# Attention plus a dense eight-expert MLP on one core: one shared ring for the factors of x, expert groups that begin with two pairs, and a planner with new engine costs

## The chip, the cores and the metric

The kernel runs on one core of a Trainium2 chip. The metric is the device time of one execution in microseconds (us). The kernel before takes 2119.99 us, the median of three runs (2118.72 to 2120.39).

The engines are named as in the profile: PE (TensorE matmuls) and PEld (its weight loads), DVE (VectorE), ACT (ScalarE), POOL (GpSimd) and SP (SyncE, which only issues DMAs here). Each works through its own queue in order and waits for the others by semaphores.

## What is computed

The input x has 2048 rows of 512. With xn the layer norm of x, the output is x + attention(xn) + experts(xn):

```python
# attention: 32 heads of 16, a window of 256 keys
qkv = xn @ wqkv
scores = q @ k.T * 16 ** -0.5         # masked to 0 <= row - key < 256
o = softmax(scores) @ v
A = o @ wo
# experts: all 8 take part (K = 8 of E = 8), F = 1376
gates = softmax(xn @ w_gate)
B = sum(gates[:, e] * (silu(xn @ w1[e]) @ w2[e]) for e in range(8))
```

All inputs are f32. The kernel splits each operand of a matmul into a high and a low half of f16 and adds three products (high by high, high by low, low by high), which the helper `mm3` issues.

## The kernel before

**Phase 0** (about the first 130 us) normalises x in four blocks of 512 rows (`tb`), projects queries, keys and values, and writes to DRAM what the second phase reads: the stacked queries and keys, the values, and the seven factors of each block of x (`XS`, 7 parts of 256 KB).

**The expert work** takes the 86 pairs of 128-column chunks of w1 and w2 in 17 *groups*. A group is two or three pairs of one expert (one group mixes chunks that lie across two experts). For a pair and a block of rows the first product, w1 by x, is one step of Strassen's method: seven products (`product`) of a combination of w1's quarters (`w`) with one factor of x (`xs`), held in two PSUM banks `zx` and `zy`, and combined by copies and additions on ACT, DVE and POOL (`s`, `za`, `zb`). Two such units run together as a *double*; `first_products` issues a double's seven products in the order p1, p2, p6, p5, p7, p3, p4. In a group of two pairs each of its four doubles is both pairs of one block of rows. In a group of three pairs, six doubles: pairs 0 and 1 of block tb, then pair 2 of blocks tb and tb + 1 (the *two-block double*), then pairs 0 and 1 of block tb + 1.

A finished unit gives two *rows* (`row`): tanh on ACT (`t`, L628), the gate of silu on DVE (L632), the high half `hh` on ACT (L643) and the low half `hl` on POOL (L646). When all rows of a group and block are there, `second` issues the second product on PE into banks `acc`, and DVE adds each bank to the output block (`x`, L568).

**The attention** runs beside it: 384 *items* of scores (`st` on PE), exponentials on ACT (`pf`, L1717), masks on POOL (L1701, L1708), high half `ph` on ACT (L1723), low half `pl` on DVE (L1727), then products with the values (`pv`). Separate products `sc` find the row maxima on DVE (L1624).

**The order on every engine is made by a planner** (`Order`) at build time. It keeps a modelled time for PE and a modelled clock for A (ACT), V (DVE), G (POOL) and S (SP). `task` queues work for an engine with a cost, dependencies and a due time; `advance` takes from each queue what can start. The PE stream asks `wait(needs)` before each product: while the needs are not met in the model, it puts other work ahead (second products, attention). The real order is what the planner emits; the real waits are by semaphores.

**Loads of x's factors.** `load_x_part` (L508 to L519) issues one part when the part it replaces has been read. Each of the seven parts has its own tag with two buffers (`xs0` to `xs6`, L517), 14 places of 2 KB per partition; a part is replaced by the same part two blocks later.

**Weights.** Each pair of w1 and w2 is loaded twice (`r`, one buffer each): once for the group's largest value (ACT, L839), once to be split and summed (`prep1`: `sums` on POOL, `w` on ACT and DVE). `hh` and `hl` have HB = 12 buffers each, w2 has 8 places.

Of the kernel before, what the change touches and what calls it, by code (L numbers as in the profile page):

```python
# [47 lines left out]
HB = 12  # L48
# [11 lines left out]
UNITS = 24000  # L60

# [19 lines left out]
class Order:  # L81
# [3 lines left out]
    def __init__(self):  # L85
        self.t = 0
        self.clock = {"A": 0, "V": 0, "G": 0, "S": 0}
        self.todo = {e: [] for e in self.clock}
        self.n = 0
        self.idle = 0  # L90
        self.strict = True

    def task(self, engine, cost, run, deps, slack, lag=0):
        ev = Event()
        self.n += 1
        self.todo[engine].append((self.t + slack, self.n, cost, lag, run, deps, ev))
        return ev
# [15 lines left out]
    def advance(self):  # L113

        while True:
            best = None
            for engine, todo in self.todo.items():
# [3 lines left out]
                for job in todo:  # L121
                    e = self.at(job[5])
                    if e is not None:
# [12 lines left out]
            self.todo[engine].remove(job)  # L136
            job[4]()
            self.clock[engine] = start + job[2]
            job[6].end = start + job[2] + job[3]
# [16 lines left out]
def tile_attn_moe(ctx: ExitStack, tc: tile.TileContext, x, wqkv, wo, _bx, wg, w1, w2, out):  # L156
# [158 lines left out]
    def prep1(g, i, r1, slot, act, dve, gps):  # L315
# [46 lines left out]
        e1 = gps(805, s1, [])  # L362
        e2 = gps(805, s2, [e1])
        h = act(500, part(a11, 0, 0, 2), [])
        w[A11] = dve(694, part(a11, 1, 0, 2), [h])
        h = act(712, part(both, 0, 6, 4), [e2])
        low = dve(867, part(both, 1, 6, 4), [h])
        w[S1] = w[S2] = low
        e4 = gps(915, s4, [e2, low])
        e3 = gps(915, s3, [e4])  # L370
        h = act(712, part(rest, 0, 2, 4), [])
        w[A12] = w[A22] = dve(904, part(rest, 1, 2, 4), [h])
        h = act(712, part(both, 0, 10, 4), [e3])
        w[S4] = w[S3] = dve(867, part(both, 1, 10, 4), [h])

    def prep2(g, i, j, r2, slot, act, dve):
# [12 lines left out]
        w["done"] = dve(838, low, [act(712, high, [])])  # L389
# [18 lines left out]
    order = Order()  # L408

# [98 lines left out]
    ahead = [0] * 7  # L508

    def load_x_part(m, free, slack):  # L510

        if ahead[m] < len(blocks):
            b = blocks[ahead[m]]
            ahead[m] += 1

            def run():
                t = moe.tile([P, 2, 2, TB // 2], F16, tag=f"xs{m}", name=f"xs{m}_{b[0]}_{b[1]}")  # L517
                nc.sync.dma_start(t, XS[b[1]][:, m])
                xs[(*b, m)] = t  # L519

            xs_at[(*b, m)] = order.move(1, run, free + ([xs_at[(*blocks[ahead[m] - 2], m)]] if ahead[m] > 1 else []), slack, LOADED)
# [20 lines left out]
    def second(g, tb, a):  # L542
# [35 lines left out]
        evicted[i_bank] = added[tb, a] = order.task("V", 746, add, deps, 6000)  # L578
# [34 lines left out]
    def row(unit, v, r, which, deps, slack):  # L613
# [31 lines left out]
        def low():  # L645
            nc.gpsimd.tensor_tensor(out=h["lo"], in0=h["t"], in1=h["hi"], op=ALU.subtract)  # L646

        before = [t_gone[-2]]
        t = order.task("A", 714, tanh, [*deps, ready[g], last_row, *before], slack)
        s = order.task("V", 805, silu, [t], slack + 1000)  # L650
        read = s
        if mixed:
            ld = order.move(2, gate_load, [gated_at[0]], slack - 3000, LOADED)
            s = order.task("V", 706, gate, [s, ld], slack + 4000)
# [4 lines left out]
        h["high"] = order.task("A", 627, high, [s, *before], slack + 2000)  # L659
        h["low"] = order.task("G", 1262, low, [h["high"]], slack + 3000)  # L660
# [23 lines left out]
    def first_products(d):  # L684
# [8 lines left out]
        def product(ps, m, n, start, stop, needs):  # L693
# [15 lines left out]
            for b in sorted({(g, tb) for g, i, tb in units}):  # L709
                if uses[b] == d:  # L710
                    load_x_part(n, [ev], 8000)
# [32 lines left out]
        def fourth():  # L744
# [9 lines left out]
        s1 = order.task("A", 588, copy(X, tile_s1), [p1, s1_gone], 2500)  # L754
        p2 = product(Y1, A12, B21, True, True, [zgone[by]])
        za0 = s1_gone = order.task(
            "V", 682, add(Y1, lambda: z_tile("a")[:, :, early], lambda: Z["s"]), [p2, s1, *reads_a], 2500
        )
        p6 = product(X, S2, T2, False, False, [s1])
        za1 = order.task("A", 588, copy(X, lambda: Z["a"][:, :, late]), [p6, za0], 2500)  # L760
        p5 = product(Y2, S1, T1, True, False, [za0])
        zb1 = order.task("V", 683, scale_y, [p5, *reads_b], 2500)
        p7 = product(X, S3, T3, False, False, [za1])
        zb0 = order.task("A", 588, copy(X, lambda: Z["b"][:, :, early]), [p7, zb1], 2500)
# [1179 lines left out]
```

## Time and profile before

| what | value |
|---|---|
| median of 3 runs | 2119.99 us |
| the profiled execution | 2119.92 us, span 2117.9 us, 2.0 us around the span |
| PE | 2093.1 us busy (99%), 16916 matmuls |
| DVE | 1625.3 us (77%) |
| ACT | 1367.1 us (65%) |
| POOL | 979.9 us (46%) |
| HBM traffic | 130 GB/s over the span |

A busy PE in this profile counts each matmul from its start to a modelled end. Successive matmuls overlap, so how fast PE works is read from the distance between starts, and what PE lost is read from its idle time and the waits that ended it. Where the text names a wait, the time is that of the engine named first, and what stands behind the arrow is what ended the wait.

### The profile page before, as it was taken

How to read it: one execution, taken by the hardware profiler on the slowest of the kernel's cores; microseconds unless marked ns; L12 is line 12 of the kernel's file. 1: busy time of each engine (PE TensorE's matmuls, PEld its weight loads, DVE VectorE, ACT ScalarE, POOL GpSimd, SP SyncE). 2: the span in 40 equal slices, each digit the busy share in tenths (PEclk: the TensorE clock that was granted, in tenths of full speed). 3: DMA queues.
4: the chain of work that ended last, by engine and by line, in shares of the span. 5: the costliest groups of instructions: out<-in, count | busy, mean ns of one | idle time of the engine just before them, and what ended most of it. 6: DMA issues, size and time to landing. Idle time of an engine off the chain costs nothing.

```text
span 2117.9 us, 44861 instructions
## 1 busy us (share of the span) xinstructions
PE 2093.1 (99%) x16916; PEld 1419.3 (67%) x16916; DVE 1625.3 (77%) x3505; ACT 1367.1 (65%) x2454; POOL 979.9 (46%) x1050
## 2 busy tenths in 40 slices
PE   7999999999999999999999999999999999999999
PEld 4656666666676667666676666666666676666674
DVE  8757787877787787778798878778787877887763
ACT  5747667666675576666666676667676666756561
POOL 4634454445352545355354535445454445444441
PEclk9999999999999999999999999999999999999999
DMA  6875444433533453434554444534444334544311
GB/s 211 282 235 176 136 132 144 118 113 110 155 106 119 130 145 106 132 101 135 158 152 145 117 131 120 149 99 137 110 129 137 107 104 116 159 127 112 78 51 50
DMA packets 287817, 279.15 MB, mean 132 GB/s; under 512 B 128328, under 2 KB 189768, under 8 KB 287600
## 3 DMA queue, kind: packets, MB, share of 16 engines
q1 hardware_dynamic: 287600, 276.28, 45.1%
q8 instruction: 133, 2.18, 0.4%
q14 instruction: 84, 0.69, 0.1%
HBM read 250.42 MB, written 25.50 MB: 130 GB/s over the span
## 4 chain that ended last, share of the span: by engine, by line
PE 94%; DVE 2%; DMA 2%; ACT 1%; issue 1%; SPq 0%; POOL 0%; DVEq 0%; POOLq 0%; ACTq 0%
PE acc L164 14%; PE acc L165 14%; PE acc L166 14%; PE zx L164 7%; PE zx L166 7%; PE zx L165 7%; PE zy L164 5%; PE zy L166 5%; PE zy L165 5%; PE st L1761 4%; PE pv L1798 3%; PE sc L1636 3%; PE qk L1342 3%; PE vg L1405 2%; DMA r<-in_B_w_dram 1%; PE wo L166 1%
## 5 line engine op out<-in xcount | busy, mean ns | idle before, releaser
L646 POOL TENSOR_TENSOR hl<-t,hh 128x512 f16<-128x512 f32 x344 | 436.8, 1278 | 348.2 <-ACT hh L643 332.2
L164 PE MATMUL acc<-w,hh 128*128 128x512 f16 x1376 | 521.1, 379 | 2.1 <-DVE x L568 2.1
L166 PE MATMUL acc<-w,hl 128*128 128x512 f16 x1376 | 521.3, 379 | 0.0
L165 PE MATMUL acc<-w,hh 128*128 128x512 f16 x1376 | 521.2, 379 | 0.0
L164 PE MATMUL zx<-xs,w 128*128 128x256 f16 x1376 | 374.8, 272 | 1.9 <-ACT s L725 1.1
L166 PE MATMUL zx<-xs,w 128*128 128x256 f16 x1376 | 374.9, 272 | 0.0
L165 PE MATMUL zx<-xs,w 128*128 128x256 f16 x1376 | 374.9, 272 | 0.0
L1717 ACT ACTIVATE pf<-st,esc 128x512 f32<-128x512 f32 (+1 forms) x384 | 251.2, 657 | 183.5 <-PE st L1761 177.7
L1624 DVE CUSTOM_DVE_ANT_0 sc<-sc,mask 128x320 f32<-128x320 f32 (+4 forms) x512 | 240.6, 474 | 136.2 <-PE sc L1636 132.4
L1727 DVE TENSOR_TENSOR pl<-pf,ph 128x512 f16<-128x512 f32 (+1 forms) x384 | 301.9, 792 | 50.1 <-ACT ph L1723 48.6
L164 PEld LDWEIGHTS <-w 128*128 128x128 f16 x2408 | 235.0, 98 | 106.2 <-DVE za L732 0.3
L165 PEld LDWEIGHTS <-w 128*128 128x128 f16 x2408 | 235.2, 98 | 95.2 <-issue 5.3
L164 PE MATMUL zy<-xs,w 128*128 128x256 f16 x1032 | 281.1, 272 | 2.5 <-DVE za L732 2.2
L166 PE MATMUL zy<-xs,w 128*128 128x256 f16 x1032 | 281.2, 273 | 0.0
L165 PE MATMUL zy<-xs,w 128*128 128x256 f16 x1032 | 281.2, 272 | 0.0
L1723 ACT ACTIVATE ph<-pf 128x512 f16<-128x512 f32 (+1 forms) x384 | 228.7, 598 | 49.2 <-POOL pf L1701 29.4
L166 PEld LDWEIGHTS <-w 128*128 128x128 f16 x2408 | 235.4, 98 | 27.4
L643 ACT ACTIVATE hh<-t 128x512 f16<-128x512 f32 x344 | 213.6, 623 | 57.7 <-DVE t L632 42.1
L1701 POOL TENSOR_SCALAR_AFFINE_SELECT pf<-pf 128x256 f32<-128x256 f32 x256 | 132.3, 518 | 249.3 <-ACT pf L1717 248.5
L166 PEld LDWEIGHTS <-hl 128*128 128x128 f16 x1376 | 134.3, 98 | 162.6
L568 DVE SCALAR_TENSOR_TENSOR x<-acc,gsc,x 128x512 f32<-128x512 f32 x256 | 190.3, 743 | 69.0 <-PE acc L166 66.8
L746 POOL TENSOR_TENSOR zb<-zb 128x512 f32<-128x512 f32 x86 | 113.6, 1321 | 230.8 <-ACT zb L725 183.9
(144 smaller groups left out, 3679.5 us busy)
## 6 DMA issues: line engine op xcount, KB each, us to landing
xs<-XS SPq DMA_DIRECT2D x476, 256.0 KB
r<-in_B_w_dram SPq DMA_DIRECT2D x172, 256.0 KB
r<-in_B_w_dram SPq DMA_DIRECT2D x80, 512.0 KB
q<-QS SPq DMA_DIRECT2D x192, 32.0 KB
VS<-vt SPq DMA_DIRECT2D x16, 272.0 KB
out_dram<-x SPq DMA_DIRECT2D x16, 256.0 KB
k<-KS SPq DMA_DIRECT2D x96, 40.0 KB
x<-in_A_x_dram SPq DMA_DIRECT2D x3, 1024.0 KB
```

Of the source, the lines that this page charges most:

```text
L164: nc.tensor.matmul(ps, lhsT=lh, rhs=rh, start=first, stop=False, **kw)
L165: nc.tensor.matmul(ps, lhsT=lh, rhs=rl, start=False, stop=False, **kw)
L166: nc.tensor.matmul(ps, lhsT=ll, rhs=rh, start=False, stop=last, **kw)
L568: nc.vector.scalar_tensor_tensor(out=dst, in0=ps, scalar=back if groups[g][0] is None else back[:, 4 * tb + a : 4 * tb + a + 1], in1=dst, ...
L643: nc.scalar.activation(out=h["hi"], in_=h["t"], func=AF.Copy)
L646: nc.gpsimd.tensor_tensor(out=h["lo"], in0=h["t"], in1=h["hi"], op=ALU.subtract)
L746: nc.gpsimd.tensor_tensor(out=zb[:, :, late], in0=zb[:, :, early], in1=zb[:, :, late], op=ALU.add)
L1624: nc.vector.tensor_tensor_reduce(out=ps[:, :n], in0=ps[:, :n], in1=maskf[:, MB * 64 - n :], scale=1.0, scalar=-3.0e38, op0=ALU.add, op1=AL ...
L1701: nc.gpsimd.affine_select(out=pf, in_=pf, pattern=[[0, 2], [1, P]], channel_multiplier=-1, base=0, compare_op=ALU.is_ge, fill=0.0,)
L1717: nc.scalar.activation(out=w["pf"][:, :n], in_=ps[:, :n], func=AF.Exp, bias=math.log(PSCALE), scale=esc)
L1723: nc.scalar.activation(out=w["hi"][:, :n], in_=w["pf"][:, :n], func=AF.Copy)
L1727: nc.vector.tensor_tensor(out=w["lo"][:, :n], in0=w["pf"][:, :n], in1=w["hi"][:, :n], op=ALU.subtract)
```

## The change

1. *One ring for x's factors.* The seven tags with two buffers become one tag `xs` with XB = 10 buffers. Parts are loaded in the order in which the products read them, block after block, and each load takes the place of the part loaded ten loads earlier. In phase 0 the 16 tiles of normalised x use the same ring.
2. *Buffers.* HB goes from 12 to 13, and w2 gets 11 places in place of 8.
3. *Groups.* Experts 0 to 6 are cut into a group of two pairs and then one of three, in place of three and then two. Expert 7 was cut so already.
4. *Low halves on either engine.* `hl` and `pl` are queued for DVE and POOL at once (`either`); the one that the model can start first takes it, and DVE only where POOL's modelled queue could not finish it in time (`in_time`).
5. *Costs.* The planner's costs for ACT, DVE, POOL and some PE work are changed (ACT's by some 100 ns each, for example tanh from 714 to 618), and a result now counts as ready LATE (80 to 100 ns) after its engine is free.

```diff
-HB = 12
+HB = 13
+XB = 10
+W2B = 11
...
+LATE = {"A": 100, "V": 80, "G": 80}
...
+    def in_time(self, job):
+
+        due, n = job[:2]
+        ahead = sum(j[2] for j in self.todo["G"] if j[:2] <= (due, n) and self.at(j[5]) is not None)
+        return max(self.clock["G"], self.at(job[5])) + ahead <= max(due, self.t + 2000)
+
+    def either(self, costs, run, deps, slack):
+
+        ev = Event()
+        self.n += 1
+        self.twins[self.n] = [
+            (engine, (self.t + slack, self.n, cost, 0, partial(run, engine), deps, ev)) for engine, cost in costs.items()
+        ]
+        for engine, job in self.twins[self.n]:
+            self.todo[engine].append(job)
         return ev
...
-                    if e is not None:
+                    if e is not None and not (engine == "V" and job[1] in self.twins and self.in_time(job)):
...
-            self.todo[engine].remove(job)
+            for e, twin in self.twins.pop(job[1], [(engine, job)]):
+                self.todo[e].remove(twin)
             job[4]()
             self.clock[engine] = start + job[2]
-            job[6].end = start + job[2] + job[3]
+            job[6].end = start + job[2] + (job[3] if engine == "S" else LATE[engine])
...
-        groups += [(e, pairs[:3]), (e, pairs[3:])] if e < E - 1 else [(e, pairs[:2]), (e, pairs[2:])]
+        groups += [(e, pairs[:2]), (e, pairs[2:])]
...
-    def load_x_part(m, free, slack):
-
-        if ahead[m] < len(blocks):
...
+    x_todo = iter([(b, m) for b in blocks for m in ORDER])
+    x_issued = Event(0)
+
+    def load_x_part(free, slack):
+
+        nonlocal x_issued
+        b, m = next(x_todo, (None, None))
+        if b is None:
+            return
+        before, x_issued = x_issued, Event()
+        here = x_issued
+
+        def run():
+            t = moe.tile([P, 2, 2, TB // 2], F16, tag="xs", bufs=XB, name=f"xs{m}_{b[0]}_{b[1]}")
+            nc.sync.dma_start(t, XS[b[1]][:, m])
+            xs[(*b, m)] = t
+            here.end = order.clock["S"] - AGO
+
+        xs_at[(*b, m)] = order.move(1, run, [*free, before], slack, LOADED)
...
-        t = order.task("A", 714, tanh, [*deps, ready[g], last_row, *before], slack)
-        s = order.task("V", 805, silu, [t], slack + 1000)
+        t = order.task("A", 618, tanh, [*deps, ready[g], last_row, *before], slack)
+        s = order.task("V", 730, silu, [t], slack + 1000)
...
-        h["high"] = order.task("A", 627, high, [s, *before], slack + 2000)
-        h["low"] = order.task("G", 1262, low, [h["high"]], slack + 3000)
+        h["high"] = order.task("A", 525, high, [s, *before], slack + 2000)
+        h["low"] = order.either({"G": 1250, "V": 740}, low, [h["high"]], slack + 3000)
...
-        s1 = order.task("A", 588, copy(X, tile_s1), [p1, s1_gone], 2500)
+        s1 = order.task("A", 492, copy(X, tile_s1), [p1, s1_gone], 2500)
...
-                for m in ORDER:
-                    load_x_part(m, [x_gone[2], xs_stored[2]] if m < 4 else [], 15000)
-                for m in ORDER:
-                    load_x_part(m, [qk_gone[1, 1], xs_stored[3]] if m < 4 else [], 30000)
+                for n in range(XB):
+                    had = 1 if n < 2 else 2 if n < 6 else 3
+                    load_x_part([qk_gone[1, 1] if had == 3 else x_gone[had], xs_stored[had]], 15000 if n < 7 else 30000)
...
-            w["low"] = order.task("V", 255 + n * 6 // 5, partial(low, n, w), [w["high"]], 7500)
+            w["low"] = order.either({"V": 140 + n * 6 // 5, "G": 200 + n * 17 // 8}, partial(low, n, w), [w["high"]], 7500)
```

**What stands where, before and after.** Both programs hold the same matmuls: 4128 into `acc`, 4128 into `zx`, 3096 into `zy`, 2880 `pv`, 992 `st`, 512 `sc`. Of the 384 `pl` operations 323 now stand in POOL's queue and 61 in DVE's; of the 344 `hl` 330 stand in POOL's and 14 in DVE's. The changed file is 30 lines longer, so L646 is L676 there, L1727 is L1757, L518 is L547.

PE's queue in the second double of all, after its third product (factor 4 of x). The names are `xs` factor_group_block and `w1` group_pair. Before, the group has three pairs, and the second double is its pair 2 of blocks 0 and 1:

```order
L166 MATMUL zx_2289<-xs4_0_1_1922,w1_0_2_2109 128x256
L1636 LDWEIGHTS q0_96
L1636 MATMUL sc_2356<-k0_98,q0_96 128x320
L1636 LDWEIGHTS q0_96
L1636 MATMUL sc_2358<-k0_98,q0_96 128x320
L164 LDWEIGHTS w1_0_2_2109
L164 MATMUL zy_2376<-xs3_0_0_1858,w1_0_2_2109 128x256
```

After, it is pairs 0 and 1 of block 1:

```order
L188 MATMUL zx_2284<-xs4_0_1_2209,w1_0_1_1958 128x256
L1666 LDWEIGHTS q0_96
L1666 MATMUL sc_2352<-k0_98,q0_96 128x320
L186 LDWEIGHTS hh_2312
L186 MATMUL acc_2356<-w2_0_0_0_1667,hh_2312 128x512
L187 LDWEIGHTS hh_2312
L187 MATMUL acc_2356<-w2_0_0_0_1667,hh_2312 128x512
L188 LDWEIGHTS hl_2313
L188 MATMUL acc_2356<-w2_0_0_0_1667,hl_2313 128x512
L186 LDWEIGHTS w1_0_0_1647
L186 MATMUL zy_2364<-xs3_0_1_2222,w1_0_0_1647 128x256
```

A group of two pairs has all rows of a block after one double, so second products (`acc`) stand inside the second double, where before there were only `sc`.

POOL's queue some 100 rows in, where the first attention items run beside the weights of group 1 (`sums`). Before:

```order
L1701 AFFINE_SELECT pf<-pf 128x2x128
L345 TENSOR_TENSOR sums<-r_1_0_2787 128x256
L348 TENSOR_TENSOR sums<-sums,r_1_0_2787 128x256
L646 TENSOR_TENSOR hl<-t,hh 128x512 x4
L1701 AFFINE_SELECT pf<-pf 128x2x128
L1708 AFFINE_SELECT pf<-pf 128x512
L351 TENSOR_TENSOR sums<-r_1_0_2787,sums 128x256
```

After:

```order
L367 TENSOR_TENSOR sums<-r_1_1_2652 128x256
L1757 TENSOR_TENSOR pl<-pf,ph 128x512
L370 TENSOR_TENSOR sums<-sums,r_1_1_2652 128x256
L1731 AFFINE_SELECT pf<-pf 128x2x128
L776 TENSOR_TENSOR zb<-zb 128x2x256
L1757 TENSOR_TENSOR pl<-pf,ph 128x512
L373 TENSOR_TENSOR sums<-r_1_1_2652,sums 128x256
L376 TENSOR_TENSOR sums<-r_1_1_2652 128x256
L676 TENSOR_TENSOR hl<-t,hh 128x512 x4
L1731 AFFINE_SELECT pf<-pf 128x2x128
```

The low halves `pl` stand between the masks, sums and `hl` on POOL; before, none did.

SP's queue at a load for a two-block double. Before, in group 2 (`xs3_2_1` replaces factor 3 of two blocks earlier):

```order
L518 DMA xs4_2_1_5073<-XS1_62 128x1024
L286 DMA r2_3_1_5078<-in_B_w2_dram 128x512 x2
L518 DMA xs3_2_1_5117<-XS1_62 128x1024
L270 DMA r1_2_2_5149<-in_B_w1_dram 128x4x256
L518 DMA xs5_2_1_5164<-XS1_62 128x1024
```

After, in group 1 (`xs3_1_1` replaces the part ten loads earlier, `xs0_1_0`):

```order
L1641 DMA v_3393<-VS_59 128x8x68
L292 DMA r1_2_0_3539<-in_B_w1_dram 128x4x256
L308 DMA r2_2_0_3541<-in_B_w2_dram 128x512 x2
L547 DMA xs3_1_1_3650<-XS1_62 128x1024
L547 DMA xs5_1_1_3700<-XS1_62 128x1024
L547 DMA xs2_1_1_3731<-XS1_62 128x1024
L547 DMA xs6_1_1_3786<-XS1_62 128x1024
```

The part `xs0_1_0` is read last by the first product of the two-block double, and `xs3_1_1` is first read by the fourth product of the same double. Between the two, PE's queue holds 36 `zx` and `zy` matmuls, 24 `pv`, 6 `sc`, 4 `st` and 3 `acc`. Before, a part and its successor lay two blocks of rows apart.

More of the change, by code (lines that the diff above doesn't have):

```diff
@@ L360, in rest @@
             return r1()[:, 2:4, :]
[L362 to L367, printed above, removed]
-        w[S1] = w[S2] = low
[L369 to L374, printed above, removed]
+        e1 = gps(780, s1, [])
+        e2 = gps(780, s2, [e1])
+        h = act(400, part(a11, 0, 0, 2), [])
+        w[A11] = dve(630, part(a11, 1, 0, 2), [h])
+        h = act(615, part(both, 0, 6, 4), [e2])
+        low = dve(880, part(both, 1, 6, 4), [h])
+        w[S1] = w[S2] = low
+        e4 = gps(900, s4, [e2, low])
+        e3 = gps(900, s3, [e4])
+        h = act(615, part(rest, 0, 2, 4), [])
+        w[A12] = w[A22] = dve(850, part(rest, 1, 2, 4), [h])
+        h = act(615, part(both, 0, 10, 4), [e3])
+        w[S4] = w[S3] = dve(880, part(both, 1, 10, 4), [h])
     def prep2(g, i, j, r2, slot, act, dve):
@@ L387, in low @@
             )
-        w["done"] = dve(838, low, [act(712, high, [])])
+        w["done"] = dve(820, low, [act(615, high, [])])
     doubles = []
@@ L408, in tile_attn_moe, with on @@
     order = Order()
+    def on(engine):
+        return nc.vector if engine == "V" else nc.gpsimd
     class Stream:
@@ L577, in second @@
         deps = [ev, added[tb, a], back_ready[g]]
-        evicted[i_bank] = added[tb, a] = order.task("V", 746, add, deps, 6000)
+        evicted[i_bank] = added[tb, a] = order.task("V", 665, add, deps, 6000)
     def append(d):
@@ L643, in high, with low @@
             nc.scalar.activation(out=h["hi"], in_=h["t"], func=AF.Copy)
-        def low():
-            nc.gpsimd.tensor_tensor(out=h["lo"], in0=h["t"], in1=h["hi"], op=ALU.subtract)
+        def low(engine):
+            on(engine).tensor_tensor(out=h["lo"], in0=h["t"], in1=h["hi"], op=ALU.subtract)
         before = [t_gone[-2]]
-        t = order.task("A", 714, tanh, [*deps, ready[g], last_row, *before], slack)
-        s = order.task("V", 805, silu, [t], slack + 1000)
+        t = order.task("A", 618, tanh, [*deps, ready[g], last_row, *before], slack)
+        s = order.task("V", 730, silu, [t], slack + 1000)
         read = s
@@ L804, in weight_tasks @@
         slots2 = [((-1,), {"gone": qk_gone[w, j]}) for w in range(2) for _ in range(2) for j in range(2)]
+        slots2 += [((-2,), None)] * (W2B - len(slots2))
         preps = {g: [] for g in range(NG)}
@@ L841, in bound @@
                         )
-                    users.append(order.task("A", 1300, bound, [ev], due + i))
+                    users.append(order.task("A", 1130, bound, [ev], due + i))
                     got += users
@@ L1723, in high, with low @@
             nc.scalar.activation(out=w["hi"][:, :n], in_=w["pf"][:, :n], func=AF.Copy)
-        def low(n, w):
-            nc.vector.tensor_tensor(out=w["lo"][:, :n], in0=w["pf"][:, :n], in1=w["hi"][:, :n], op=ALU.subtract)
+        def low(n, w, engine):
+            on(engine).tensor_tensor(out=w["lo"][:, :n], in0=w["pf"][:, :n], in1=w["hi"][:, :n], op=ALU.subtract)
         def ratio(pv, box):
@@ L1770, in att_out @@
             t = last_exp = order.task(
-                "A", 260 + n * 5 // 6, partial(exp, ps, n, w), [order.pe(28 + n * 3 // 7), last_exp, *old], 2500
+                "A", 160 + n * 5 // 6, partial(exp, ps, n, w), [order.pe(n * 7 // 16), last_exp, *old], 2500
             )
@@ L1801, in att_out @@
                         )
-                ev = order.pe(30 * 4 * len(kbs))
+                ev = order.pe(25 * 4 * len(kbs))
                 for i in ns:
@@ L1843, in low @@
                 )
-            t = order.task("V", 689, low, [order.task("A", 593, high, [ev, oh_gone], 3000)], 4000)
+            t = order.task("V", 610, low, [order.task("A", 500, high, [ev, oh_gone], 3000)], 4000)
             until(t)
```

38 lines of the change are left out of this document (16 added, 22 removed).

## The prediction

> **What bounds the kernel now.** I read the page first, then PE's waits, then the timeline at each of them.
>
> ```profile
> span 2117.9 us, 44861 instructions
> PE 2093.1 (99%) x16916; PEld 1419.3 (67%) x16916; DVE 1625.3 (77%) x3505; ACT 1367.1 (65%) x2454; POOL 979.9 (46%) x1050
> PE   7999999999999999999999999999999999999999
> PEclk9999999999999999999999999999999999999999
> ```
>
> PE is busy everywhere but in the first fortieth, at full granted clock. Busy alone can hide a slow stream, so the distance between starts must be seen too (timeline of PE: start, duration, line):
>
> ```profile
> 999.82 0.27 PE L164 MATMUL zy<-xs,w 128*128 128x256 f16 x1
> 999.92 0.27 PE L165 MATMUL zy<-xs,w 128*128 128x256 f16 x1
> 1000.47 0.38 PE L164 MATMUL acc<-w,hh 128*128 128x512 f16 x1
> 1000.69 0.38 PE L165 MATMUL acc<-w,hh 128*128 128x512 f16 x1
> ...
> 1001.12 0.30 PE L1636 MATMUL sc<-k,q 128*128 128x320 f16 x1
> 1001.25 0.27 PE L164 MATMUL zx<-xs,w 128*128 128x256 f16 x1
> ...
> 1635.84 0.18 PE L1798 MATMUL pv<-v,ph 128*128 128x34 f16 x1
> 1635.86 0.18 PE L1798 MATMUL pv<-v,pl 128*128 128x34 f16 x1
> ```
>
> From start to start a matmul of 256 columns takes some 0.11 us, one of 320 0.13, one of 512 0.22, and a `pv` of 34 about 0.025: the time goes with the columns, and the forms chain without a hole. Since both programs hold the same matmuls, only idle time of PE can be won or lost: 2117.9 − 2093.1 = 24.8 us. Where it lies (stretch, its length, busy time and count of PE, PEld, DVE, ACT and POOL, clock, DMA share, GB/s):
>
> ```profile
> 0.00:20.00 20.00, 8.78 (x47) 5.53 (x48) 15.94 (x58) 9.12 (x22) 7.30 (x19) 1.00 0.80 264
> 150.00:190.00 40.00, 35.60 (x279) 26.22 (x277) 26.75 (x63) 27.59 (x50) 15.88 (x18) 1.00 0.67 201
> ```
>
> and who PE waited for from 60 us on (us in total, times, longest):
>
> ```profile
> PE zy L164 <- DVE za L732: 2.2, 2, 1.3
> PE acc L164 <- DVE x L568: 2.1, 1, 2.1
> PE zx L164 <- ACT s L725: 1.1, 1, 1.1
> PE zx L164 <- ACT za L725: 0.7, 1, 0.7
> PE wo L166 <- DVE ol L1841: 0.7, 1, 0.7
> PE wo L164 <- DVE x L1856: 0.6, 1, 0.6
> PE sc L1636 <- ACT s L725: 0.5, 1, 0.5
> ```
>
> The first 20 us lose 11.2 us and the stretch from 150 to 190 us 4.4 us. The waits shown sum to 7.9 us. So a change that leaves the first 20 us alone can win about 8 us, 0.4%, and no more.
>
> **The change part by part.** The sum is made on the profiled execution, 2119.9 us, which is the median of the runs within 0.1 us.
>
> *Groups of two pairs lead.* The waits near 160 us, in PE's timeline:
>
> ```profile
> 156.64 0.27 PE L164 MATMUL zx<-xs,w 128*128 128x256 f16 x1 [1.13 <-ACT s L725]
> 159.52 0.27 PE L164 MATMUL zy<-xs,w 128*128 128x256 f16 x1 [1.27 <-DVE za L732]
> 171.02 0.27 PE L164 MATMUL zy<-xs,w 128*128 128x256 f16 x1 [0.95 <-DVE za L732]
> 173.68 0.27 PE L164 MATMUL zx<-xs,w 128*128 128x256 f16 x1 [0.73 <-ACT za L725]
> ```
>
> The first two lie in the first double, whose queue is the same after the change; I keep both. The last two lie in the second double, where before only `sc` could stand between dependent products. Now second products stand there, 3 × 0.22 = 0.65 us each, so these 0.95 + 0.73 = 1.7 us go. Bounds: nothing (the first `hl` may come too late for its new place, which would put a wait of like size there) and 1.7 us. I take −1.7. The other groups have cover from second products before and after, and cost nothing.
>
> *Low halves move to POOL.* Two rows give the price (groups: count | busy us, mean ns | idle before):
>
> ```profile
> L646 POOL TENSOR_TENSOR hl<-t,hh 128x512 f16<-128x512 f32 x344 | 436.8, 1278 | 348.2 <-ACT hh L643 332.2
> L1727 DVE TENSOR_TENSOR pl<-pf,ph 128x512 f16<-128x512 f32 (+1 forms) x384 | 301.9, 792 | 50.1 <-ACT ph L1723 48.6
> ```
>
> A `pl` on POOL has the shape of `hl`. POOL gains a net 309 operations × 1.28 = 395 us, from 980 to about 1375 us (65%). DVE loses 309 × 0.79 = 243 us, from 1625 to about 1380 us (65%). Neither is the bound. What can be won is PE's waits on a late DVE, and the longest late wait shows how one comes about (chain of waits; start, duration):
>
> ```profile
> 1634.06 1.35 POOL hl L646
> 1636.96 2.38 POOL sums L351
> 1641.25 1.56 DVE t L632
> 1643.48 0.67 DVE x L568
> ```
>
> and PE's timeline at its end:
>
> ```profile
> 1644.19 0.38 PE L164 MATMUL acc<-w,hh 128*128 128x512 f16 x1 [2.07 <-DVE x L568]
> ```
>
> POOL was late first, DVE's `t` waited and then ran long, and the `x` behind it freed PE's bank 2 us late. Fewer operations on DVE help here, more on POOL hurt. Of the four late waits on DVE and ACT (2.1 + 0.7 + 0.6 + 0.5 = 3.9 us) I take half as gone: −2.0. Bounds: −3.9, and a new one of 2.1 us at several groups (a rival below).
>
> Why POOL and DVE are not free of each other (duration minimum/median/maximum in ns, by tile):
>
> ```profile
> L646 POOL TENSOR_TENSOR hl<-t,hh x344: 1148/1162/1956, 168.0 to 2094.0; 128x512 f16<-128x512 f32 x172
> L632 DVE SCALAR_TENSOR_TENSOR t<-t,zb x172: 652/689/1660, 171.3 to 2092.1; 128x512 f32<-128x512 f32 x172
> L568 DVE SCALAR_TENSOR_TENSOR x<-acc,gsc,x x256: 708/745/753, 190.7 to 2114.1; 128x512 f32<-128x512 f32 x128
> ```
>
> DVE's `t`, with both inputs in SBUF, takes 0.65 to 1.66 us; `x`, with one input in PSUM, always 0.71 to 0.75. The Trainium skill (SBUF — State Buffer, "SBUF: two separate sides") says that a DVE operation with two SBUF inputs and a GpSimd operation that reads SBUF exclude each other for a whole instruction. The trace agrees: the spread of `t`, 1.0 us, is most of one `hl`. By that rule a `pl` moved to POOL shuts DVE out for 1.16 us where it used to occupy DVE for 0.69; what this would do is the second slower rival.
>
> *The ring.* Before, a part's successor was needed two blocks later, tens of us. Now, in each two-block double (9 groups of three pairs, 18 doubles), parts are loaded while the double runs. At the place shown in the order, the time between release and need is PE's work there: 36 × 0.11 + 24 × 0.025 + 6 × 0.13 + 4 × 0.11 (`st`, also 256 columns) + 3 × 0.22 = 6.4 us; counted through the order in the same way, 64 loads have under 9 us and the shortest 6.0 us. Against it stand, from the chain (issue to use):
>
> ```profile
> 129.02 3.89 DMA xs<-XS
> 146.81 6.93 DMA r<-in_B_w_dram
> ```
>
> and from SP's timeline, the first and the last of one attention burst of 14 issues:
>
> ```profile
> 1036.58 0.50 SPq L137 DMA_DIRECT2D k<-KS  x1
> 1045.43 0.39 SPq L1611 DMA_DIRECT2D v<-VS  x1
> ```
>
> A part landed 3.9 us after its issue, a weight tile twice its size 6.9 us, and SP needs 8.9 us for the burst. With 3.9 us the load is hidden by 2 us. Behind a burst or beside a weight load it isn't, by up to 6.9 − 6.0 = 0.9 us. Behind a load that lands late PE itself is queued, with all that follows in its order. Bounds: 0, and 0.9 us in 18 doubles, 16 us. I take 0.5 us, since most of these loads stand behind one another and not behind a burst.
>
> *Costs, HB, W2B.* They issue nothing. Where the old costs held ACT's results (tanh 714) the new ones hold 618 + 100, the same moment; but the engine counts as free 100 ns earlier per operation. So the plan is closer to the chip, and PE's needs are placed less late than before. At 200 to 1000 us no PE wait of 0.5 us stood in the trace; that cover shrinks. By the nearest row, one wait of 1.1 us as in the first double in a tenth of 86 doubles would be 9.5 us; the lower bound is 0. I take 1.2, nearer zero, since ACT's operations hardly vary and only those of DVE and POOL do.
>
> *Start.* On DVE one `mxw` reduction moves ahead of the first layer norm, into the 0.36 us in which DVE waits for ACT's root, and one fewer follows it. Its two ends, 0.3 us later and 0.3 us earlier, cancel: 0.
>
> Sum: −1.7 − 2.0 + 0.5 + 1.2 + 0 = −2.0, so 2117.9 us.
>
> **The rivals.** This kernel's runs tell a difference of 0.2%, 4.2 us, from none: faster is below 2115.8, slower above 2124.2.
>
> *The cover holds everywhere.* All waits of the list but the first double's 1.13 + 1.27 go, 7.9 − 2.4 = 5.5 us, or the first double is helped too, 7.9 us, and nothing comes in: 2112 to 2114.4, say 2113. For it: DVE, behind most of those waits, has 15% less to do. Against it: every lead gets shorter at once.
>
> *The ring is late.* Place: SP's queue ahead of the fourth product of a two-block double. It decides from a landing later than 6.0 us after release. At 0.9 us in 18 doubles, 16.2 us, less the 3.7 won: 2119.9 + 12.5 = 2132; in half of them, 2124.3. For it: the weight load's 6.9 us. Against it: the part's 3.9.
>
> *POOL shuts DVE out.* Place: a group's weight preparation, where `sums`, `hl` and now `pl` stand in POOL's queue and `t` on DVE waits. Its price is the 2.1 us seen once in 17 groups; it decides where five or more groups show it: 5 × 2.1 = 10.5, less 1.7: about 2128.7. For it: the rows of `t`, and POOL at 65%. Against it: DVE has gaps again, and `x` and `za` read PSUM.
>
> That the low halves stay where they were is ruled out by the order (323 of 384 moved).
>
> **How the numbers follow.** No change: 0.44, its own range 2115.8 to 2122. Cover everywhere: 0.35. Ring late: 0.11; POOL shuts DVE out: 0.10. The predicted time is the likeliest's, 2117.9. The range takes in the faster rival down to its 2111, and of the slower ones the half up to 2128. Faster 0.35, same 0.44, slower 0.21.
>
> **What would show it.** Right: PE's waits at 170 us gone, those in the first double kept; DVE near 1380 us and POOL near 1375; PE's waits after 200 us in sum between 2 and 7 us. Wrong: waits of PE on the transfer into `xs` (the ring); `t`'s mean far above its 0.8 us with PE waits on `x` or `za` behind it (the shared port); many waits of `zx` or `zy` on ACT's or DVE's copies at 0.3 us or more (cover lost); or fewer than 2 us after 200 us (the faster rival).

## The result and the profile after

The changed kernel takes 2147.1 us (median of four runs, 2142.9 to 2150.3) against 2119.6 us before: ratio 1.0129, 95% interval 1.0106 to 1.0151, so 27.5 us slower. The forecast was 2117.9 us. The profiled execution took 2144.28 us, with a span of 2142.5. The head of its page:

```profile
span 2142.5 us, 44823 instructions
PE 2101.7 (98%) x16916; PEld 1420.2 (66%) x16916; DVE 1507.1 (70%) x3196; ACT 1364.3 (64%) x2454; POOL 1326.2 (62%) x1359
PE   7999999999999999999999999999999999999999
PEclk9999999999999999999999999999999999999999
```

The matmuls are the same 16,916. PE is idle for 2142.5 − 2101.7 = 40.8 us in place of 24.8, and its busy time is 8.6 us longer. The tenths of the page hide both. Busy time can grow because a start that comes late, but before the modelled end of the matmul ahead of it, leaves no idle time. To see where it went, the same stretches of both kernels side by side, first of the kernel before, then of the change (stretch, its length, busy time and count of PE, PEld, DVE, ACT, POOL, clock, DMA share, GB/s):

```profile
0.00:200.00 200.00, 183.27 (x1208) 117.21 (x1209) 141.17 (x348) 122.64 (x287) 92.84 (x110) 1.00 0.72 231
200.00:1000.00 800.00, 800.00 (x6584) 547.74 (x6582) 621.13 (x1369) 531.18 (x921) 377.99 (x406) 1.00 0.44 126
```

```profile
0.00:200.00 200.00, 182.55 (x1188) 116.44 (x1189) 141.70 (x353) 121.19 (x285) 98.35 (x111) 0.99 0.74 237
200.00:1000.00 800.00, 792.27 (x6478) 538.86 (x6478) 574.51 (x1222) 522.01 (x909) 508.51 (x517) 1.00 0.44 123
1132.00:1135.56 3.56, 1.45 (x11) 0.86 (x10) 3.56 (x4) 1.93 (x4) 3.39 (x3) 1.00 0.15 48
1135.56:1138.97 3.41, 3.41 (x15) 2.16 (x14) 3.41 (x5) 1.67 (x3) 1.16 (x1) 0.50 0.10 13
```

From 200 to 1000 us PE never stood still before; now it idles 7.7 us there and gets through 106 fewer matmuls. The first 200 us lose little more than before. From each start on PE to the next, those that took over 60 ns longer than the median behind a matmul of the same form were 48, 21.7 us too long in sum, and are now 109, 45.4 us in sum. That makes 23.7 of the 24.6 us between the spans. The loss is many short waits, spread over the whole program. Whom PE waited for from 60 us on (us in total, times, longest):

```profile
PE zy L186 <- DVE za L762: 5.3, 6, 2.1
PE sc L1666 <- DMA q<-QS: 2.5, 1, 2.5
PE mx L889 <- DVE m L313: 2.3, 1, 2.3
PE mT L1673 <- DVE mt L1654: 2.1, 3, 1.0
PE zx L186 <- ACT s L755: 2.1, 3, 1.2
PE zx L186 <- ACT za L755: 1.7, 2, 1.1
PE acc L188 <- POOL hl L676: 1.7, 2, 1.2
```

All waits of the whole list, of which these are the first rows, sum to 23.5 us in 30 places, against 8.8 us in 11 before. Most, 13.9 us, are on DVE. No wait on a transfer into `xs` is among them. How one of them comes about, on POOL's and on DVE's timeline, and what PE then does:

```profile
1130.68 3.16 POOL L1757 TENSOR_TENSOR pl<-pf,ph 128x512 f16<-128x512 f32 x2
1133.80 1.60 POOL L676 TENSOR_TENSOR hl<-t,hh 128x512 f16<-128x512 f32 x1
```

```profile
1131.84 0.99 DVE L668 TENSOR_TENSOR t<-t,gb 128x512 f32<-128x512 f32 x1
1132.75 1.64 DVE L662 SCALAR_TENSOR_TENSOR t<-t,zb 128x512 f32<-128x512 f32 x1
1134.31 0.68 DVE L762 SCALAR_TENSOR_TENSOR za<-zy,s 128x512 f32<-128x512 f32 x1
```

```profile
1135.04 0.27 PE L186 MATMUL zy<-xs,w 128*128 128x256 f16 x1 [2.11 <-DVE za L762]
1135.81 0.42 PE L186 MATMUL zy<-xs,w 128*128 128x256 f16 x1
1136.02 0.42 PE L187 MATMUL zy<-xs,w 128*128 128x256 f16 x1
```

Two `pl` and an `hl` stand on POOL, each at 1.6 us. Beside them DVE's two operations with both inputs in SBUF take 0.99 and 1.64 us, where the planner's new costs have 0.70 and 0.73. The `za` behind them is late, and PE stands for 2.11 us. Then the granted clock falls to one half for 3.41 us (the last row of the stretches above): matmuls of 256 columns start 0.21 us apart in place of 0.11. Such a stretch costs some 1.7 us (an estimate: half of its 3.41 us). There are two in this execution, at 173.0 and 1135.6 us, and none inside the profiled execution of before: 3.4 of the 24.6 us between the spans.

### The profile page after: what moved, and what is told of

It reads as the page before. It is cut to its first block, busy times and chain, and to the rows that moved or that the text cites. A ratio compares the mean times of both kernels' runs of the same rounds, so it can differ in the third digit from the quotient of the medians.

```text
span 2142.5 us, 44823 instructions
## 1 busy us (share of the span) xinstructions
PE 2101.7 (98%) x16916; PEld 1420.2 (66%) x16916; DVE 1507.1 (70%) x3196; ACT 1364.3 (64%) x2454; POOL 1326.2 (62%) x1359
## 4 chain that ended last, share of the span: by engine, by line
PE 83%; DVE 7%; DMA 3%; ACT 2%; POOL 2%; issue 2%; SPq 1%; DVEq 0%; ACTq 0%; POOLq 0%
PE acc L186 12%; PE acc L188 12%; PE acc L187 12%; PE zx L186 6%; PE zx L188 6%; PE zx L187 6%; PE zy L186 4%; PE zy L188 4%; PE zy L187 4%; PE qk L1373 4%; PE pv L1828 3%; PE st L1791 3%; PE sc L1666 3%; PE vg L1436 2%; DVE t L662 2%
## 5 line engine op out<-in xcount | busy, mean ns | idle before, releaser
L676 POOL TENSOR_TENSOR hl<-t,hh 128x512 f16<-128x512 f32 x330 | 423.0, 1292 | 187.8 <-ACT hh L673 173.6
L1757 POOL TENSOR_TENSOR pl<-pf,ph 128x512 f16<-128x512 f32 (+1 forms) x323 | 376.4, 1170 | 125.7 <-ACT ph L1753 121.0
L187 PEld LDWEIGHTS <-w 128*128 128x128 f16 x2408 | 235.4, 98 | 98.0 <-issue 12.2
```

Source lines behind the costliest of these rows:

```text
L187: nc.tensor.matmul(ps, lhsT=lh, rhs=rl, start=False, stop=False, **kw)
L676: on(engine).tensor_tensor(out=h["lo"], in0=h["t"], in1=h["hi"], op=ALU.subtract)
L1757: on(engine).tensor_tensor(out=w["lo"][:, :n], in0=w["pf"][:, :n], in1=w["hi"][:, :n], op=ALU.subtract)
```

## The experiments

Theories. **Cover**: the new modelled costs and `LATE` let the planner place PE's needs closer behind the engines that feed them, so that small delays reach PE. **Low halves**: POOL's new work makes POOL late or shuts DVE out. **Groups** and **ring**: the order of the groups, or shorter leads of loads. **Order**: each edit reshuffles the whole plan, and the kernel before has an unusually good one. Each difference below is between a kernel's median and the median of the kernel before, measured together with it; the intervals of the ratios are some ±3 us wide for most.

### One part of the change taken back

```diff
 no_costs:  every modelled cost as before, no LATE
 no_either: -h["low"] = order.either({"G": 1250, "V": 740}, low, ...)   +h["low"] = order.task("G", 1250, low, ...)
            -w["low"] = order.either({"V": ..., "G": ...}, ...)         +w["low"] = order.task("V", 140 + n * 6 // 5, ...)
 no_groups: -(e, pairs[:2]), (e, pairs[2:])   +(e, pairs[:3]), (e, pairs[3:])   (but for the last expert)
 no_ring:   -tag="xs", bufs=XB   +tag=f"xs{m}";  HB 13 -> 12, W2B 11 -> 8
```

> The change with all modelled costs as they were before (of PE too) and without LATE; groups of two, either and ring stay. If the new costs took away the planner's cover, most of the 24 us come back: 2119 to 2128 us, and PE's waits after 200 us fall from about 20 us to under 8. If the low parts on GpSimd or the ring are the cause, it stays at 2140 to 2150 us. If the loss is made of equal shares of all four parts, 2138 to 2143.

> The change with pl on VectorE and hl on GpSimd as before; new costs, groups of two and ring stay. If the move of the low parts is the cause (GpSimd late, or VectorE shut out while GpSimd reads), 2118 to 2126 us, with the mean of t back from 0.89 to 0.80 us and of w from about 1.03 to 0.89. If the new costs are the cause, VectorE has still less slack and it is no better than the change: 2143 to 2152 us. If the ring is, 2140 to 2150.

> The change with the groups as before (three pairs lead). If the order of the groups brought the loss, 2119 to 2128 us. Otherwise 2140 to 2152: the waits in the second double that the prediction took away, 1.7 us, come back and nothing else moves beyond some us of scatter.

> The change with the parts of x in seven tags of two buffers as before, HB 12 and eight places for second weights; new costs, either and groups of two stay. If the ring's shorter leads and the order of loads on the queue are the cause, 2118 to 2127 us. If the new costs or the low parts are, 2139 to 2150, since no wait of PE on a transfer into xs stands in the trace of the change.

Measured: without the new costs 2126.6 us, 9.0 over before (ratio 1.0042, 1.0027 to 1.0057), so 18.5 of the 27.5 us come back. Without `either` 2140.7 (+23.1), without the groups 2143.4 (+25.8), without the ring 2135.1 (+17.5). Waits of PE after 60 us fall to 12.5 us without the costs; with the three others they stay at 19.5 to 21.6. By this test the costs are the largest part. The ring, with HB and W2B, returns 10 us, which lies between the two ranges expected; the low halves 4.4 and the groups 1.7, which is about what the intervals can tell.

### The costs of one engine taken back

```diff
 old_dve: -"V": 730, 665, 606, 740, 140 + 6/5 n ...  +805, 746, 682, 805, 255 + 6/5 n ...;  LATE["V"] = 0
 old_act: -"A": 618, 525, 492, 160 + 5/6 n ...       +714, 627, 588, 260 + 5/6 n ...;       LATE["A"] = 0
 old_pe:  -pe(25 * 4 * len(kbs)), pe(n * 3 // 7) ... +pe(30 * 4 * len(kbs)), pe(n // 2) ...
```

> The change (2147 us) with VectorE's modelled costs alone as before (t 805, pl 255 + 1.2 n, za 682 and so on) and VectorE's LATE at 0; the rest of the change stays. In the trace of the change VectorE is busy for 1507 us, while its new modelled costs sum to 1388 us: t takes 0.89 us on the chip and 0.73 in the plan. If the plan runs ahead of the real VectorE and that is the loss, most of the 20 us come back that all old costs together gave: 2125 to 2132 us. If ScalarE's or TensorE's costs are the cause, it stays at 2141 to 2150.

> The change with ScalarE's modelled costs alone as before (tanh 714, copies 588, exp 260 + n 5/6) and ScalarE's LATE at 0. The moment at which one result counts as ready is the same as in the change; only a following operation may start 0.1 us earlier. If this occupancy was the cover, 2125 to 2132 us and PE's waits on ScalarE's s, za, zb (3.8 us) are gone; if not, 2141 to 2150.

> The change with TensorE's modelled costs alone as before (pv 30 per column block, sc n/2, st 28 + 3 n/7). They add 34 us to the modelled time of attention's matmuls, 2124 in place of 2090 us in sum. If a modelled PE that is slower than the real one gives away cover (its products are then planned too late, and other engines seem to be done sooner than they are), the time rises to 2147 to 2155. If it gives cover, 2125 to 2135.

For DVE and ACT the cost goes up by about what LATE goes down, so a result counts as ready at nearly the same moment (805 in place of 730 + 80), and only the engine's next operation starts later in the plan. Measured: 2142.7 (+24.8), 2146.5 (+28.7) and 2143.2 us (+25.4). No single engine is the guilty one: none differs clearly from the change's +27.5. The waits of PE after 60 us show where the loss went. First with DVE's costs as before, then with ACT's:

```profile
PE zy L186 <- DVE za L762: 3.7, 7, 1.1
PE sc L1666 <- ACT pf L1747: 2.5, 2, 1.5
PE acc L186 <- ACT hh L673: 2.5, 1, 2.5
```

```profile
PE sc L1666 <- DMA q<-ZERO: 5.3, 3, 2.3
PE sc L1666 <- DVE mt L1654: 4.4, 6, 2.0
PE acc L188 <- POOL hl L676: 3.1, 3, 1.4
```

With DVE's longer operations back in the plan, the waits on DVE fall from 13.9 to 9.6 us and those on ACT rise from 4.3 to 8.8. With ACT's, those on ACT fall to 2.8 us and those on POOL and on attention's loads rise from 4.9 to 8.4. In these two executions the waits moved to the other engines, and their sum hardly fell (21.3 and 22.8 us in place of 23.5). And waits are not all: with ACT's costs the granted clock fell to one half six times, for 20.5 us in sum, in place of 6.8.

### Cover by one number

`AGO` is the margin of the planner: a result may be used that many ns after its modelled end.

```diff
 after_ago200:  (the change)         -AGO = 100   +AGO = 200
 before_ago200: (the kernel before)  -AGO = 100   +AGO = 200
```

> The change (2147 us) with one number of the planner raised: each result may be used 200 ns after its modelled end in place of 100 (AGO). This gives back, on every engine at once, about the 0.1 us that the new costs took from each operation, and leaves the costs themselves, the groups, the low parts and the ring. If lost cover at the hand-offs is the cause, 2125 to 2135 us and PE's waits after 60 us fall from 23.5 us to 10 to 15. If it is not the margin but the proportion of the costs to each other, 2142 to 2150.

> The kernel before with the margin at 200 ns, as in the run of the change with 200 (2128 us). If more cover takes away waits, the remaining 8.8 us of PE's waits after 60 us shrink and it is faster than before: 2111 to 2117 us. If the kernel before stands at an unusually good order and any new one loses more than cover gives, 2120 to 2130.

The change with 200 takes 2128.1 us (+9.1): 18.4 us come back, as much as with all old costs, and with every new cost in place. So more room at every hand-off makes up for what the new costs took, whatever their proportions. That it is the same room is not shown: the new costs left the moment at which a result counts as ready nearly as it was and freed the engine 0.1 us earlier. And the kernel before with 200 takes 2149.9 us (+31.7), against both expectations. Its loss has another place (the stretches of its trace, and PE's timeline in it):

```profile
130.00:200.00 70.00, 50.71 (x346) 29.53 (x343) 47.48 (x126) 34.72 (x63) 24.27 (x27) 0.83 0.45 136
200.00:1000.00 800.00, 797.30 (x6426) 543.23 (x6427) 610.51 (x1291) 514.56 (x895) 373.78 (x392) 1.00 0.44 127
139.57 1.01 PE L1483 MATMUL gp<-ident,gates 128*8 128x128 f32 x4 [4.26 <-DVE gates L1462]
187.46 0.42 PE L1636 MATMUL sc<-k,q 128*128 128x320 f16 x1 [2.43 <-ACT pf L1717]
189.15 0.19 PE L1798 MATMUL pv<-v,ph 128*128 128x34 f16 x1 [1.27 <-DVE mt L1624]
```

At the passage from phase 0 to the experts PE waits 4.26 us for the gates, and from 174.5 us on it works through attention items with little else between them. It is idle for 19.3 of 70 us at a mean clock of 0.83. Of its late starts 28.4 us lie between 100 and 200 us (5.7 before), and 14.0 us after 200 us (5.7 before). Part of this is clock: five stretches of half clock make 34.1 us, in which PE is busy for 24.9, so some 12 us of the 31.7 (an estimate: half of the busy time). So more margin is no remedy as such: with the same operations it cost the one plan about what the whole change costs, and took two thirds of the loss from the other. Why the plan puts attention alone at that place was not tested.

### One part of the change alone

```diff
 only_costs:  (the kernel before) + all new modelled costs + LATE
 only_either: (the kernel before) + order.either for hl and pl, at the old costs
 only_ring:   (the kernel before) + tag="xs", bufs=10; HB 12 -> 13, W2B 8 -> 11
 only_groups: (the kernel before) + groups of two pairs lead
```

> The kernel before with all the new modelled costs and LATE and nothing else: pl on VectorE, hl on GpSimd, three pairs lead, seven tags of two. If the new costs alone carry the loss, 2132 to 2145 us; if they only do harm with the ring or the moved low parts, 2117 to 2125.

> The kernel before with the low parts on VectorE or GpSimd by queues, at the old costs (pl 319 of 384 on GpSimd), and nothing else. My prediction's term was -2.0 us, so 2115 to 2117. If GpSimd shuts VectorE out and that costs time by itself, t's mean rises from 0.80 to 0.89 us and the time to 2122 to 2128. If VectorE has room for it at the old costs, 2115 to 2119.

> The kernel before with the ring of ten places, HB 13 and eleven places for second weights, at the old costs, and nothing else. My term was +0.5 us: 2118 to 2121. The change without its ring ran 12 us faster than the change, so by that the ring costs 5 to 12 us: 2123 to 2130, with waits of PE on products whose part of x or whose place in the queue came late.

> The kernel before with groups of two pairs leading and nothing else. My term was -1.7 us: the waits of 0.95 and 0.73 us at 171 to 174 us go, 2115 to 2117. If the first low part comes too late for its new place, a wait of PE on hl stands near 180 us and the time is 2118 to 2122.

Measured: costs +16.8 (2134.7 us), `either` +12.2 (2131.2), ring +20.7 (2139.7), groups +8.1 (2127.2). Each alone makes the kernel slower, `either`, ring and groups by more than expected. They do not add: 57.8 us in sum, 27.5 together. The run without the costs holds the last three at the old costs, and there they make 9.0 us, where they sum to 41.0 alone. So none of these figures is a part's share of the 27.5. DVE's groups with both inputs in SBUF, and `x` with one in PSUM, in the kernel before, with `either` alone, in the change without `either`, in the change, and in the change without the new costs (count | busy us, mean ns | idle before):

```profile
L632 DVE SCALAR_TENSOR_TENSOR t<-t,zb 128x512 f32<-128x512 f32 x172 | 144.6, 844 | 11.7 <-ACT t L628 11.3
L632 DVE SCALAR_TENSOR_TENSOR t<-t,za 128x512 f32<-128x512 f32 x172 | 128.7, 758 | 20.5 <-ACT t L628 20.0
L384 DVE SCALAR_TENSOR_TENSOR w<-r,sc,w 128x512 f16<-128x512 f32 x86 | 73.5, 863 | 3.0 <-ACT w L381 2.9
L568 DVE SCALAR_TENSOR_TENSOR x<-acc,gsc,x 128x512 f32<-128x512 f32 x256 | 190.3, 743 | 69.0 <-PE acc L166 66.8
```

```profile
L654 DVE SCALAR_TENSOR_TENSOR t<-t,za 128x512 f32<-128x512 f32 x172 | 145.7, 856 | 46.3 <-ACT t L650 40.9 <-POOL pf L1730 1.4 <-POOL pl L1749 0.9
```

```profile
L640 DVE SCALAR_TENSOR_TENSOR t<-t,za 128x512 f32<-128x512 f32 x172 | 123.6, 729 | 33.7 <-ACT t L636 33.0
```

```profile
L662 DVE SCALAR_TENSOR_TENSOR t<-t,za 128x512 f32<-128x512 f32 x172 | 142.4, 834 | 58.9 <-ACT t L658 55.9 <-POOL pf L1738 1.9 <-POOL zb L776 0.3
L662 DVE SCALAR_TENSOR_TENSOR t<-t,zb 128x512 f32<-128x512 f32 x172 | 162.5, 949 | 24.3 <-ACT t L658 24.0
L406 DVE SCALAR_TENSOR_TENSOR w<-r,sc,w 128x512 f16<-128x512 f32 x86 | 87.2, 1020 | 5.4 <-ACT w L403 5.4
L598 DVE SCALAR_TENSOR_TENSOR x<-acc,gsc,x 128x512 f32<-128x512 f32 x256 | 190.8, 745 | 148.9 <-PE acc L188 147.3
```

```profile
L661 DVE SCALAR_TENSOR_TENSOR t<-t,zb 128x512 f32<-128x512 f32 x172 | 169.5, 988 | 26.5 <-ACT t L657 23.9 <-POOL hl L675 2.1
L661 DVE SCALAR_TENSOR_TENSOR t<-t,za 128x512 f32<-128x512 f32 x172 | 151.0, 888 | 34.6 <-ACT t L657 33.1 <-POOL pl L1756 0.4
```

The move of `pl` makes each of 172 `t` on `za` 0.1 us longer (0.73 and 0.76 without it, 0.83 and 0.86 with it), and `w` on `r` takes 1.02 us in the change (0.86 before); the new costs of these two are 0.73 and 0.82. `x` stays at 0.74 to 0.75 us. But longer operations are not lost time by themselves: without the new costs `t` takes 0.89 and 0.99 us, more than in the change, and 18.5 of the 27.5 us are gone; without `either` it is back at 0.73 and 0.87 us, and 23.1 of the 27.5 us stay. How much of the 12.2 us is longer operations, and how much the new order, is not told apart.

With the groups alone, PE's timeline and the stretch behind it:

```profile
139.10 0.60 PE L1483 MATMUL gp<-ident,gates 128*8 128x128 f32 x4 [3.39 <-DVE gates L1462]
139.71:143.12 3.41, 3.41 (x9) 1.18 (x8) 2.63 (x5) 1.86 (x4) 1.48 (x2) 0.50 0.27 88
```

The wait on the gates and the half clock behind it make 3.4 + 1.7 = 5.1 of the 8.1 us, at a place where the prediction expected nothing. What the prediction did expect of the groups came: of the four waits in the first two doubles, 4.1 us in sum before, there remain two, of 0.65 and 0.21 us, and no wait on `hl` stands there.

### What in the ring costs

```diff
 ring14:       (only_ring) -XB = 10, HB = 13, W2B = 11   +XB = 14, HB = 12, W2B = 8
 ring10_small: (only_ring) -HB = 13, W2B = 11            +HB = 12, W2B = 8
```

> The kernel before with the ring, but of fourteen places, the room that the seven tags of two had, with HB 12 and eight places for second weights as before. The ring of ten alone cost 21 us (2139.7). If its shorter leads cost that, in the chip's transfers or in the planner, which holds a product until its part's modelled landing, this one is at 2117 to 2122 us. If one common order of loads costs it, 2130 to 2140.

> The kernel before with the ring of ten places and HB 12 and eight places for second weights as before, so that only the number of places differs from the run with fourteen, and only HB and W2B from the run with the ring alone (2139.7). If ten places in place of fourteen cost the 21 us, 2134 to 2142. If the room given to HB and W2B costs them, by weights prepared earlier and at other moments, 2118 to 2125.

Measured: fourteen places +4.9 (1.0025, 1.0016 to 1.0035), ten places +8.6, ten places with the larger HB and W2B +20.7. So the ring's form costs 4.9, the fewer places 3.7 more (within the intervals), and **12.1 us come with HB and W2B** (a difference of two runs, each with its own ±3 us). The stretch from 200 to 1000 us, first with the ring, HB and W2B, then with the ring alone:

```profile
200.00:1000.00 800.00, 793.37 (x6441) 539.96 (x6440) 616.25 (x1320) 517.87 (x898) 370.50 (x395) 1.00 0.43 124
```

```profile
200.00:1000.00 800.00, 797.74 (x6532) 543.42 (x6530) 625.62 (x1345) 520.93 (x909) 376.30 (x399) 1.00 0.43 123
```

Where weights have more room PE gets through 91 matmuls fewer. PE's waits on transfers into `xs` are 0.8 and 1.5 us over the whole execution. Which of HB and W2B it is was not tried.

### Is it the order as such?

```diff
 before_tanh718: (the kernel before)  -order.task("A", 714, tanh, ...)   +order.task("A", 718, tanh, ...)
 before_ago110:  (the kernel before)  -AGO = 100   +AGO = 110
 after_ago110:   (the change)         -AGO = 100   +AGO = 110
```

> The kernel before with one modelled cost raised by 4 ns (tanh 714 to 718): no term of any theory, but the planner's order differs from some way into the program on. If the kernel before stands at an unusually good order and any new order loses, 2123 to 2132 us with PE's waits after 60 us at 12 to 18 us in place of 8.8. If each of the four parts has its own cost of 8 to 21 us, this one has none: 2116 to 2120.

> The kernel before with the planner's margin at each hand-off at 110 ns in place of 100: cover grows by 10 ns, the order changes from the start on. If any new order loses, 2123 to 2132 us; if only the four parts' own effects count, 2115 to 2120.

> The change with the margin at 110 ns in place of 100. It shows how far orders of the same kernel scatter. If the loss of the change is a bad draw of the order, this one draws again: anywhere from 2128 to 2150. If the new costs make every order worse by some 15 us, 2138 to 2150 like the change itself.

Measured: 2120.0 us (+1.7; 1.0010, 1.0001 to 1.0019), 2120.9 (+2.6; 1.0017, 1.0007 to 1.0026) and 2146.2 (+28.0). Two thousand rows and more on DVE stand in another order in the first two, and they cost 2 to 3 us. So a small push to the order costs little, twice, and another order of the change is no better than the first. That a larger push costs more for no other reason is not ruled out: the new costs alone and the margin of 200 also change nothing but the order, and cost 16.8 and 31.7 us, and every larger edit of the kernel before that was tried made it slower. None of the 18 kernels is faster than the kernel before. All of them in one table:

| kernel | median us | minus before | PE's waits after 60 us: us, times |
|---|---|---|---|
| the change | 2147.1 | +27.5 | 23.5, 30 |
| no_costs | 2126.6 | +9.0 | 12.5, 21 |
| no_either | 2140.7 | +23.1 | 19.5, 31 |
| no_groups | 2143.4 | +25.8 | 21.6, 30 |
| no_ring | 2135.1 | +17.5 | 20.5, 31 |
| old_dve | 2142.7 | +24.8 | 21.3, 36 |
| old_act | 2146.5 | +28.7 | 22.8, 24 |
| old_pe | 2143.2 | +25.4 | 22.1, 33 |
| after_ago200 | 2128.1 | +9.1 | 16.0, 22 |
| after_ago110 | 2146.2 | +28.0 | 28.0, 39 |
| only_costs | 2134.7 | +16.8 | 17.6, 23 |
| only_either | 2131.2 | +12.2 | 15.2, 24 |
| only_ring | 2139.7 | +20.7 | 20.9, 32 |
| ring10_small | 2126.6 | +8.6 | 12.0, 23 |
| ring14 | 2122.9 | +4.9 | 8.6, 13 |
| only_groups | 2127.2 | +8.1 | 14.3, 19 |
| before_tanh718 | 2120.0 | +1.7 | 7.5, 11 |
| before_ago110 | 2120.9 | +2.6 | 8.6, 14 |
| before_ago200 | 2149.9 | +31.7 | 24.6, 24 |

## Why the prediction was wrong

It had the right frame: the same matmuls at nearly full clock, at most 8 us to win, and everything else a question of PE's waits. That only idle time can be won or lost was not quite right: PE's busy time grew by 8.6 us, 3.4 of them by half clock. It was wrong in the size of four terms, and in their signs where it forecast a gain. (One side reading was off as well: the time goes with the columns from 256 up, but a `pv` of 34 starts 0.025 us behind the last, where the columns alone would give 0.015.)

- **Costs, HB, W2B: +1.2, bounds 0 to 9.5. This is the step that failed most.** The mechanism was named (PE's needs are placed less late, "that cover shrinks"), and its sign came; the size did not. The costs alone measure +16.8, taken back 18.5, and the margin at 200 gives 18.4. The upper bound came from one kind of wait, 1.1 us, on the copies in a tenth of the doubles. What came are short waits on every kind of hand-off, among them attention's scores and maxima (`sc`, `mT`), the weights' maxima (`mx`) and the second products, and half-clock stretches behind some of the longer ones. That ACT's operations hardly vary did not keep the loss small: 13.9 of the 23.5 us of waits are on DVE, and ACT's old costs by themselves gave nothing back. Of HB and W2B the prediction said that they issue nothing. That is true, and it left their effect on the plan at zero, where 12.1 us were measured beside the ring.
- **Low halves: −2.0.** Alone they measure +12.2; taken back from the change, 4.4. DVE was to fall to about 1380 us and is at 1507: the rows of `t` and `w` above are longer than before (`t` 0.83 and 0.95 us in place of 0.76 and 0.84), which the sum left out, although the rival that POOL shuts DVE out rested on the same rows. POOL is at 1326 us, against 1375. That rival's 2128.7 us is near what the part does alone (2131.2), but by luck as far as the runs show: its price was one wait of 2.1 us in five groups' weight preparation, and the stretch at 1131 us shows `pl`, `hl` and `t` of ordinary work. That `t` and `w` get longer beside POOL's reads is what the Trainium skill (SBUF — State Buffer, "SBUF: two separate sides"), cited in the prediction, would have by its exclusive lock for operations with two SBUF inputs; the rows agree, `x` with one input in PSUM staying at 0.74 to 0.75 us.
- **The ring: +0.5.** Its rival, parts that land late ahead of the fourth product, did not come in the change: no PE wait on `xs` is in its trace. The ring's own cost is 4.9 to 8.6 us with the old HB and W2B. With ten places 1.5 of the 12.0 us of waits are on `xs`; with fourteen none is, and the waits are no longer than before (8.6 us against 8.8). Where those 4.9 us lie is open but for one stretch of half clock at 174.5 us, some 1.7 us.
- **Groups: −1.7.** With the groups alone the waits of 0.95 and 0.73 us in the second double went, as forecast, and so did those of the first double, which were to stay; other waits outweighed both. In the whole change others came at the same place. PE's timeline of the change:

```profile
171.14 0.27 PE L889 MATMUL mx<-ident,m 128*2 128x128 f32 x1 [2.31 <-DVE m L313]
172.56 0.27 PE L186 MATMUL zx<-xs,w 128*128 128x256 f16 x1 [1.15 <-ACT za L755]
```

  They sum to 3.5 us in place of 1.7, with a half-clock stretch behind them. Without the new costs the wait on `mx` is not there, so it is not the groups' own. A term that removes a wait has to ask what PE's next need is at that place.
- **PE's waits after 200 us** were to sum to 2 to 7 us; they sum to 18.6 in 26 places (4.2 in 5 before). The sign set for the lost cover, many waits of 0.3 us or more on the copies and on `za`, is what came.

What stays open: why the parts do not add, and so how the 27.5 us divide among them; whether the kernel before merely stands at a plan that any larger push makes worse; how the 12.2 us of the low halves divide between longer operations and the new order; and through which wait the room for HB and W2B acts.

## What to carry to other kernels

In a program that a planner orders, its cost table sets the spacing of every hand-off. Here costs nearer to the undisturbed intervals (tanh: 0.618 us in place of 0.714, where its starts lie 0.61 us apart back to back) cost some 17 to 18 us, though results counted as ready at nearly the same moment, and no engine's costs alone gave it back. So price such an edit from the slack at all hand-offs, not from one kind of wait. Whether costs taken from the mean under load would do better was not tried; DVE's old costs, which are nearer to that mean, gave back 2.7 us, within the intervals. Then vary the margin by itself: 200 in place of 100 gave one plan 18.4 us and cost the other 31.7, so a margin that suits one plan says nothing of the next. And take one part back as well as trying it alone, since the two need not agree (the ring with HB and W2B: 10.0 us back, 20.7 alone).

## What the hardware showed beyond that

A single wait of PE can be paid twice. In the change a wait of 2.11 us, with PE busy for 1.45 of 3.56 us, was followed by 3.41 us at half clock; with the groups alone a wait of 3.39 us did the same, and the kernel before at the margin of 200 has a stretch of 13.65 us at half clock from 179.35 us on. But the wait of 2.48 us at 1212 us in the change, and that of 2.07 us at 1644 us before, had no such effect.

The traces show what makes the difference. In all 20 of them the changes of the granted clock lie whole multiples of 3.413 us apart. On that grid the wait of 2.11 us falls into one window, in which PE is busy for 1.31 of 3.41 us. The waits of 2.48 and 2.07 us each fall across a border: their windows are busy for 2.50 and 1.85 us, and for 2.31 and 2.46. Taken over all traces up to 2100 us, of the windows at full clock in which PE was busy for under 0.40 of the time, 19 of 19 were followed by half clock; from 0.40 to 0.52, 12 of 19; above, 1 of 12,142. So a short wait costs more or less by where it falls on this grid, whose place against the kernel's start differs from trace to trace. It also shows in the scatter: the change's fastest execution, 2142.9 us, has a mean granted clock of 0.999, its slowest, 2150.3 us, one of 0.996.

The Trainium skill (TensorE: Matmul & The Clock Gate, "Part 1: The HAM clock gate (the "warmup" mystery)") tells of a free-running window of some 3.4 us whose activity sets the clock to a half or to full; the traces agree, with stretches of 3.41 us or multiples and one grid in each trace. The Trainium skill's rule ("HAM oscillation — how this bites in real kernels") to have no idle gaps above about 3.4 us is too mild by these rows: 2.11 us was enough.
